# Attention into a routed expert layer: value rows copied by DMA instead of VectorE, and the first expert products planned together with the attention

## The chip, the cores and the metric

One core of a Trainium2 chip runs the whole program. The metric is the time of one execution on the device in microseconds, the median of several runs. Engines are named as in the profile: PE (TensorE), DVE (VectorE), ACT (ScalarE), POOL (GpSimd) and SP (SyncE, which only issues DMAs here).

## The reference, cut to what matters

The program has three parts in a row: an attention with a window, a layer of 8 experts of which each token uses one, and a gated layer. The change touches the first and the seam to the second.

```python
# attention: B, H, S, D = 4, 8, 768, 64; n_global, n_local = 8, 96
keep = (key < n_global) | ((rel >= 0) & (rel < n_local))      # rel = query - key
scores = where(keep, scale * q @ k.T + bias, -1e9)            # bias falls with the distance
a = exp(scores - max); a = a / (sum(a) + 1e-9)
x = (a @ v) laid out as [3072 tokens, 512]
# experts: w1 is [8, 512, 1024], w2 is [8, 1024, 512]
logits = x @ w_gate;  expert_idx = argmax;  gate_w = its softmax probability
out[tokens of e] = gate_w * (relu(x_e @ w1[e]) @ w2[e])
# then: sigmoid(out @ w_gate2) * (out @ w_val) @ w_out
```

A query sees the first 8 keys and the 96 keys up to itself, so a tile of 128 queries needs the 8 global keys, 96 or more keys of the tile before it, and its own 128.

## The kernel before, in words

**Attention.** `attention` (L457) works through 24 tiles of 128 queries, 6 for each of 4 batches (tile t is row block i = t % 6 of its batch), each in two halves s = 2t and 2t + 1 of four heads. Per tile SP loads k, q and v (L489, L497); PE transposes k and q (T, L523); ACT or DVE copies them out of PSUM (TH, L534, L536). Per half, PE makes the scores (QK, L556), DVE adds the bias and takes the row's extreme (TTR, L566), ACT exponentiates (EXP, L583), PE transposes the weights (PT, L595), ACT and DVE (or POOL) split them into two float16 parts (PHI L608, PLO L621), PE multiplies with the values (PV, L636 to L638), ACT moves the result out of PSUM (PO, L644) and POOL divides by the sum (NM, L664; the last two halves on DVE). POOL splits the values themselves into two float16 parts of `V[t]` (VP, L506 to L511).

**The old tile's value rows.** PV of a tile with i > 0 multiplies with two value tiles: `V[t-1]` and `V[t]`. In `V[t-1]` the first 32 rows must hold something else than the old keys: 24 rows of zeros (with a constant in row 0) and the 8 global rows. The kernel keeps them ready in `spec`, filled by one small DMA on ACT's queue per batch (in PO, L642), and DVE copies these 32 rows over the first 32 rows of `V[t-1]` (VB, L516), 20 times in all, before the tile's first PV.

**Routing in attention.** After a tile's two NM, PE transposes the rows (X, L674), ACT and DVE split them (XE L680, XL L683), PE multiplies with the gate's weights (L, L690), and a chain of small DVE, ACT and PE operations (MX, MB, EW, EX, MW, OH, CUM, POS, SL, EP, SI, RR) finds each token's expert and its place in that expert's list. OH (L729) is the one-hot row of the chosen expert; CUM (L732) adds it to the running counts, POS (L736, L737) multiplies with it. RR stores the tile's rows to DRAM (L756, SP), SC scatters its token numbers into the lists (L759, POOL).

**The head.** After tile 18 (`HEAD`), HC and HS find the expert that has most tokens so far, HV has SP read its number, load the first 256 token numbers of its list (L1005) and the first quarter of its weights (L1024); HG gathers those token rows (POOL, L1052); XG (L1064), XP (L1075), XA (L1086) and XD (L1090) scale, transpose and split them; WH (L1031) and WL (L1038) split the weights.

**The planner.** `plan` (L400) is a list scheduler in Python: from `graph`'s dependences, `COST`, `HOP`, `LAG` and a fixed priority `RANK` per kind of operation it simulates five engines and emits all operations in the order of their simulated starts. Every engine is a queue in order, so this order decides who waits behind whom. Loads of tile t + 2 are emitted by hand ahead of the first operation of tile t; so are the clears of DRAM buffers (L187 to L194).

**The seam.** The plan ends with the last tile's NM. The rest of that tile's routing is not planned: `g.tail` holds it in three pieces, which `ffn` calls around the first product `mm1(0, 0)`, along with the split of the second quarter of the weights (on POOL for p < 2, L1031). The loads of the second and third quarter are issued by hand at SC of tile 21. `ffn` then runs 9 items (two of 256 tokens for the first expert, then one for each other expert) in 8 steps each. A step is one group of 12 matmuls of `mm1` (L1140; ACT and DVE turn it into two float16 parts, L1144, L1145) and one of `mm2` (L1157); `mm1` of step n + 1 is emitted ahead of `mm2` of step n. At n = 2 `routing` finds all lists' lengths, at n = 2 and 3 the token numbers and rows of item 1 are fetched, which needs the last tile's scatter.

Of the kernel before, what the change touches and what calls it, by code (L numbers as in the profile page):

```python
# [8 lines left out]
F32 = mybir.dt.float32  # L9
# [11 lines left out]
E = 8  # L21
# [122 lines left out]
def constants(tc, g, tmp):  # L144
# [58 lines left out]
UNIT = dict(  # L203
    ND="D", NS="A", T="P", GC="G", QK="P", TTR="D", EXP="A", PT="P", PHI="A", PLO="D", PV="P",
    PO="A", SM="G", RC="D", NM="G", PG="G", HC="P", HS="D", HV="S", HG="G", XG="D", WH="G", WL="D", XP="P", XA="A", XD="D", X="P", XE="A", XL="D", L="P", MX="D", MB="D", EW="D", EX="A", MW="D", OH="D", CUM="D", POS="P",
    SL="D", EP="D", SI="D", RR="D", SC="G", VP="G", VB="D",
)
COST = dict(
    T=0.438, GC=0.21, PV=0.364, PO=0.268, SM=0.29, RC=0.09, NM=0.585, PG=0.59, X=0.438,
    XE=0.478, XL=0.6, L=0.303, MX=0.075, MB=0.29, EW=0.135, EX=0.244, MW=0.073, OH=0.3, CUM=0.19, POS=0.055,  # L210
    SL=0.075, EP=0.3, SI=0.073, RR=0.075, SC=1.17, VB=0.4, HC=0.03, HS=1.04, HV=0.01, HG=1.3, XG=0.6, WH=1.01,
    WL=1.3, XP=0.5, XA=0.478, XD=0.605,
)
SMALL = dict(MB=0.075, EP=0.075, OH=0.17, CUM=0.075, SM=0.09)
# [5 lines left out]
    T=-585.54, TH=-103.10, GC=-1092.71, QK=342.11, TTR=729.21, EXP=758.03, PT=347.71, PHI=1.34, PLO=247.24,  # L220
    PV=-729.22, SM=723.51, PO=130.74, RC=441.88, NM=-435.94, X=-229.91, XE=-436.15, L=386.67, MX=2161.16,
    EW=1001.43, EX=-1348.91, MW=105.77, OH=-1379.26, CUM=165.73, POS=-352.27, SL=-1123.54, EP=402.59, SI=-2894.64,
    RR=-1471.08, SC=328.83, VP=716.58, VB=-1236.17, HC=547.55, HS=-1259.72, HV=-973.76, HG=-355.21, XG=-407.53,
    WH=952.70, WL=1888.62, XP=-481.22, XA=-1266.94, XD=26.01, XL=776.35, MB=-892.16, PG=58.37, ND=-2151.11,
    NS=-1641.63,
)
PACE = 8.9592
ASIDE = ((1, 1), (3, 1))
DIRECT = ()
THU = ("AA", "AD")  # L230
LAG = dict(HS=1.0, HV=8.5, HG=5.0)
HEAD = 18
# [14 lines left out]
def graph():  # L247
# [13 lines left out]
    for t in range(NTILE):  # L261
# [12 lines left out]
        add(("VP", t, 2), [("VP", t, 1)], cost=1.12)  # L274
        if i:
            add(("VB", t), [("PV", 2 * t - 1, 1)] + ([("PO", 2 * t - 2)] if i == 1 else []))
            add(("GC", t), [("TH", t - i, 0), ("QK", 2 * t - 2), ("QK", 2 * t - 1)])
        for s in (2 * t, 2 * t + 1):
            add(
                ("QK", s), [("TH", t, 0), ("TH", t, 1)] + ([("GC", t)] if i >= 1 else []),  # L280
                bank=("S", 2), cost=0.93 if i else 0.57,
# [13 lines left out]
            for z in range(2):  # L295
# [11 lines left out]
                else:  # L307
# [4 lines left out]
                    [("PLO", s, z), ("VP", t, 2)] + ([("VB", t)] if i else []) + ([("PV", s, 0)] if z else []),  # L312
# [15 lines left out]
        if t == NTILE - 1:  # L328
            break
# [5 lines left out]
        add(("MB", t), [("MX", t)])  # L335
# [3 lines left out]
        add(("OH", t), [("MW", t)])  # L339
        prev = [("CUM", t - 1)] if t else []  # L340
        add(("CUM", t), [("OH", t)] + prev)
        add(("POS", t), [("OH", t), ("EX", t)] + prev)
        add(("SL", t), [("POS", t)], [("L", t, 0)])
        add(("EP", t), [("EX", t)])
# [6 lines left out]
    add(("HV", t), [("HS", t), ("SC", t)])  # L351
    for z in range(2):
        add(("HG", t, z), [("HV", t)])
        add(("XG", t, z), [("HG", t, z)])
        add(("WH", t, z), [("HV", t)])
        add(("WL", t, z), [("WH", t, z)])
# [25 lines left out]
def plan():  # L382
# [3 lines left out]
    def rank(k):  # L386
# [3 lines left out]
        r = PACE * k[1] + RANK[op]  # L390
        if op in ("T", "TH"):
            return r + 3.0 * k[2]
# [16 lines left out]
    lands = {("T", 0): 4.1, ("T", 1): 5.8, ("VP", 0): 7.3, ("ND", 128): 4.6}  # L409
# [45 lines left out]
def attention(ctx, tc, g):  # L455
# [12 lines left out]
    spec = [v_p.tile([G0 + NG, H, 130], F16, name=f"spec{n}", bufs=1) for n in range(2)]  # L468
# [15 lines left out]
    def load(t):  # L484
        b, i = tiles[t]
        rows = slice(i * 128, (i + 1) * 128)
        for src, dst, nm in ((g.k, kn, "kn"), (g.q, qn, "qn")):
            x = dst[t] = qk_p.tile([128, H, D], F32, tag=nm, name=nm)
            nc.sync.dma_start(out=x, in_=src[b, :, rows, :].rearrange("h p d -> p h d"))  # L489
            if t == 0 and nm == "kn":  # L490
                for n, a in enumerate((g.n_global, g.n_local)):
                    nc.sync.dma_start(
                        out=g.raw[:, n, :],
                        in_=a.rearrange("(o n) -> o n", o=1).bitcast(U32).to_broadcast([128, 2]),
                    )
# [3 lines left out]
    def VP(bank, t, z):  # L499
        b, i = tiles[t]  # L500
        if z == 0:
            if t < 2:
                nc.gpsimd.memset(spec[t].bitcast(F32), 0.0)
                nc.gpsimd.memset(spec[t][0:1, :, D : D + 1], 1.0 / PSC)
# [118 lines left out]
    def PV(bank, s, z):  # L623
# [5 lines left out]
        srcs = [V[t]] if i == 0 else [V[t - 1], V[t]]  # L629
# [10 lines left out]
    def PO(bank, s):  # L640
        if s % (2 * NB) == 0:
            nc.scalar.dma_start(out=spec[s // (2 * NB) % 2][G0:], in_=V[s // 2][:NG])  # L642
# [153 lines left out]

    def WH(bank, t, z):
        moe.whigh(z, 0)

    def WL(bank, t, z):  # L800
        moe.wlow(z, 0)
# [7 lines left out]
    def XD(bank, t, z):  # L809
# [5 lines left out]
        HC=HC, HS=HS, HV=HV, HG=HG, XG=XG, WH=WH, WL=WL, XP=XP, XA=XA, XD=XD, VP=VP, VB=VB, ND=lambda bank, w: distance(w), NS=lambda bank, w, qd: slopes(w, qd),  # L815
# [9 lines left out]
    for op, *at, bank in plan()[0]:  # L825
        if op == "VP" and at[0] >= 2 and at[1] == 0:
            clear(at[0] - 2)
        if op == "SC" and at[0] == NTILE - 3:
            tmps.close()
            moe.open("mw", 1)  # L830
            for p in range(1, 3):
                moe.wload(0, p)
                moe.wload(1, p)
# [4 lines left out]
    z = NTILE - 1  # L838

    def tail(*ops, bank=None):  # L840
        for f in ops:
            f(bank, z)
# [1180 lines left out]
```

## Time and profile before

| | us |
|---|---|
| median of 3 runs | 1010.46 (1010.03 to 1010.9) |
| profiled execution, its own time | 1016.85 |
| its span, first to last instruction | 1015.0 |
| PE busy | 966.7 (95%) |
| DVE busy | 740.2 (73%) |
| ACT busy | 513.8 (51%) |
| POOL busy | 432.8 (43%) |

The shares are means over stages with different limits: attention fills about the first 196 us, the experts go to about 505 us, the gated layer takes the rest. PE's busy time is modelled and counts each matmul's pipeline, so a PE at 95% is not at its peak.

### The profile page before, as it was taken

The numbers are of one execution on the slowest core, as the hardware profiler recorded it, in microseconds if no ns is written. First come the engines' busy times: TensorE is split into PE (matmuls) and PEld (weight loads), VectorE is DVE, ScalarE is ACT, GpSimd is POOL, SyncE is SP. The second block draws the span as 40 slices with busy tenths as digits, with TensorE's granted clock in tenths as the row PEclk, the third lists the DMA queues.
The fourth block names the chain that finished last, engine by engine and source line by source line (L and its number), as shares of the span: only waits on it lengthen the run. The fifth ranks groups of instructions, "written<-read, shape, count | busy, mean of one in ns | idle before, by whom it ended". The sixth has DMA issues, their size and how long they took to land.

```text
span 1015.0 us, 20665 instructions
## 1 busy us (share of the span) xinstructions
PE 966.7 (95%) x7793; PEld 678.8 (67%) x7793; DVE 740.2 (73%) x1625; ACT 513.8 (51%) x987; POOL 432.8 (43%) x537
## 2 busy tenths in 40 slices
PE   7999999689999999999999999999999999999994
PEld 5878777577555556666555588666876668766683
DVE  5999989965678789876867698445974459644693
ACT  6999989535556566656544453222621137121440
POOL 8878878640333335333778812224022240222102
PEclk9999999999999999999999999999999999999997
DMA  9877693367899999996677635552355514554031
GB/s 198 210 174 179 148 213 94 94 192 230 264 291 272 322 312 290 327 342 215 186 247 258 216 130 226 177 185 95 131 205 205 183 56 172 198 188 160 1 125 67
DMA packets 165699, 197.33 MB, mean 194 GB/s; under 512 B 88547, under 2 KB 129910, under 8 KB 165590
## 3 DMA queue, kind: packets, MB, share of 16 engines
q1 hardware_dynamic: 159990, 181.73, 57.5%
q0 software_dynamic: 5008, 14.11, 4.4%
q8 instruction: 63, 1.03, 0.4%
q14 instruction: 46, 0.38, 0.1%
q10 hardware_dynamic: 592, 0.08, 0.1%
HBM read 146.81 MB, written 49.23 MB: 193 GB/s over the span
## 4 chain that ended last, share of the span: by engine, by line
PE 41%; DVE 8%; issue 3%; DMA 2%; ACT 0%; another core or an unknown queue 0%; SPq 0%; POOLq 0%; POOL 0%; DVEq 0%; ACTq 0%
PE q L1370 30%; PE p L1455 10%; DVE h L1348 2%; DVE wk L1360 2%; PE acc L1157 1%; PE hp L1140 1%; DMA raw<-in_moe_w_gate_dram 1%; DVE wl L1038 1%; DVE yo L1290 1%; DMA raw<-yT 1%; DVE wk L1357 1%; DVE h L1417 0%; DMA wy<-wz 0%; DVE h L1403 0%
## 5 line engine op out<-in xcount | busy, mean ns | idle before, releaser
L1370 PE MATMUL q<-yo,set 128*128 128x384 f16 x2016 | 330.7, 326 | 2.8 <-DVE h L1417 2.8
L1370 PEld LDWEIGHTS <-set 128*128 128x128 f16 x2016 | 197.2, 98 | 135.1 <-issue 6.0
L1455 PE MATMUL p<-wy,wk 128*128 128x256 f16 x1404 | 154.1, 273 | 0.2 <-DVE wk L1357 0.2
L1455 PEld LDWEIGHTS <-wk 128*128 128x128 f16 x1404 | 137.3, 98 | 16.7 <-DVE wk L1357 0.4
L1140 PE MATMUL hp<-xT,wh 128*128 128x256 f16 (+7 forms) x576 | 136.6, 323 | 2.9 <-ACT xT L1086 1.5
L1421 POOL TENSOR_TENSOR h<-h,t 128x384 f32<-128x384 f32 x60 | 59.1, 998 | 152.3 <-DVE t L1417 137.2
L1391 ACT ACTIVATE u<-q 128x384 f32<-128x384 f32 x48 | 23.1, 482 | 161.1 <-PE q L1370 147.5
L1538 POOL DMA_INDIRECT out_dram<-o,idt x24 | 23.6, 983 | 178.2 <-DVE o L1506 122.9
L1140 PE MATMUL hp<-xT,wl 128*128 128x256 f16 (+7 forms) x288 | 93.3, 324 | 3.4 <-DVE wl L1038 3.3
L1038 DVE SCALAR_TENSOR_TENSOR wl<-wr,wh 128x1024 f16<-128x1024 f32 x64 | 84.3, 1317 | 14.8 <-ACT wh L1033 6.8
L1157 PE MATMUL acc<-hl,wh 128*128 128x256 f16 (+7 forms) x288 | 93.0, 323 | 0.2 <-DVE hl L1145 0.2
L1157 PE MATMUL acc<-hh,wh 128*128 128x256 f16 (+7 forms) x288 | 93.0, 323 | 0.0
L1157 PE MATMUL acc<-hh,wl 128*128 128x256 f16 (+7 forms) x288 | 93.0, 323 | 0.0
L1423 ACT ACTIVATE h<-h 128x384 f32<-128x384 f32 x72 | 37.4, 521 | 103.6 <-DVE h L1417 77.3
L583 ACT ACTIVATE pp<-tt,mall 128x232 f32<-128x232 f32 (+1 forms) x192 | 81.7, 474 | 4.1 <-DVE mall L566 4.0
L1157 PEld LDWEIGHTS <-wh 128*128 128x128 f16 x576 | 56.6, 98 | 35.2
L1140 PEld LDWEIGHTS <-wh 128*128 128x128 f16 x576 | 56.6, 99 | 34.2 <-issue 1.7
L1393 DVE TENSOR_TENSOR u<-q,u 128x384 f32<-128x384 f32 x48 | 26.8, 558 | 67.6 <-PE q L1370 67.6
L1144 ACT ACTIVATE hh<-hp 128x256 f16<-128x256 f32 (+7 forms) x72 | 34.5, 479 | 81.4 <-PE hp L1140 73.8
L566 DVE CUSTOM_DVE_ANT_0 tt<-s,nb 128x232 f32<-128x232 f32 (+1 forms) x192 | 64.2, 368 | 7.7 <-PE s L556 5.8
L1145 DVE SCALAR_TENSOR_TENSOR hl<-hp,hh 128x256 f16<-128x256 f32 (+7 forms) x72 | 39.1, 543 | 41.0 <-ACT hh L1144 40.1
L970 POOL TENSOR_TENSOR parts<-pair,parts 128x512 f16<-128x512 f32 (+1 forms) x24 | 34.2, 1424 | 72.5 <-ACT parts L969 72.5
(215 smaller groups left out, 1941.3 us busy)
## 6 DMA issues: line engine op xcount, KB each, us to landing
wr<-in_moe_w_dram SPq DMA_DIRECT2D x64, 512.0 KB
set<-us SPq DMA_DIRECT2D x36, 896.0 KB
wy<-wz SPq DMA_DIRECT2D x28, 768.0 KB
us<-set SPq DMA_DIRECT2D x12, 896.0 KB
kn<-in_k_dram SPq DMA_DIRECT2D x24, 256.0 KB
qn<-in_q_dram SPq DMA_DIRECT2D x24, 256.0 KB
vn<-in_v_dram SPq DMA_DIRECT2D x24, 256.0 KB
raw<-in_moe_w_gate_dram SPq DMA_DIRECT2D x12, 512.0 KB
```

Source lines behind the costliest of these rows:

```text
L566: nc.vector.tensor_tensor_reduce(out=tt[s][:, j, :w], in0=S_[s][j % 2][:, j // 2, :w], in1=g.nb[w][:, h, :], scale=-0.125, scalar=3.0e38, ...
L583: nc.scalar.activation(pp[s][:, j, 256 - w :], tt[s][:, j, :w], AF.Exp, bias=g.mall[:, t, h : h + 1], scale=-1.0)
L970: nc.gpsimd.tensor_tensor(lo, x[:, b : b + k, :], hi, op=ALU.subtract)
L1038: self.tc.nc.vector.scalar_tensor_tensor(lo, self.raws.pop((z, p)), WS[z], hi, op0=ALU.mult, op1=ALU.subtract)
L1140: nc.tensor.matmul(bk, a[:, k, fs], b[:, k, :], start=(m == 0), stop=(m == 11))
L1144: nc.scalar.activation(hh, bk, AF.Relu)
L1145: nc.vector.scalar_tensor_tensor(hl, bk, 0.0, hh, op0=ALU.max, op1=ALU.subtract)
L1157: nc.tensor.matmul(acc[i][dk], a[:, f % 2, d], b, start=(f == 0 and m == 0), stop=(f == NF - 1 and m == 2))
L1370: nc.tensor.matmul(bk, w[:, za, a, us], self.y[zy][:, y, u, :], start=(start and n == 0), stop=(n == 5), skip_group_check=not start,)
L1421: (V if last else G).tensor_tensor(at(half, tok), at(half, tok), d, op=ALU.mult)
L1423: A.activation(d, d, AF.Sigmoid, scale=1.0 / (YS * AS[0]))
L1455: nc.tensor.matmul(bks[t], w[:, za, j, 128 * t : 128 * t + 128], y[:, j, zy, :], start=(new and j == 0 and m == 0 and t != 1), stop=(j == ...
```

## The change

- VB is gone, and so is `spec`. Three buffers `prev` of 128 rows hold the zeros, the constant and the 8 global rows for good (POOL memsets at tiles 0, 1 and 2), and a new operation VC on SP copies rows 32 to 127 of `V[t]` into `prev[t % 3]` by DMA (20 times, 96 rows of 2080 bytes). For i < 3 a second DMA of 8 rows brings the global rows. PV reads `prev[(t-1) % 3]` in place of `V[t-1]`.
- OH is a `tensor_tensor` of two tensors, where it was a `tensor_scalar` with a column as scalar.
- The loads of `n_global` and `n_local` move from SP's queue (behind the first k) to ACT's queue (ahead of the gate's weights).
- The last tile's routing is planned; `g.tail` is gone.
- `HEAD` is 16. New planned operations: MO (closes the temporary pool, loads the second quarter of the weights), WH and WL for that quarter (WH on ACT), MW2 (loads the third quarter), and M1, HH and HL, the first 4 `mm1` groups of item 0 with their two float16 parts, into a pool `early`. `ffn` leaves these out and begins with `mm2(0, 0)`.
- The planner's costs and priorities change, with a second set `RANKL` for tiles from 20 on; QK's cost, for one, goes from 0.93 to 1.0.

```diff
@@ tables
+    for n, a in enumerate((g.n_global, g.n_local)):
+        nc.scalar.dma_start(
+            out=g.raw[:, n, :], in_=a.rearrange("(o n) -> o n", o=1).bitcast(U32).to_broadcast([128, 2])
+        )
     g.wl = tmp.tile([128, KD, E], F32, name="wl")
@@ constants of the plan
-LAG = dict(HS=1.0, HV=8.5, HG=5.0)
-HEAD = 18
+LAG = dict(HS=1.0, HV=8.5, HG=5.0, MO=9.0, VC=3.5)
+HEAD = 16
+PRE = 4
@@ graph
+        if i < NB - 1:
+            add(("VC", t), [("VP", t, 2)] + ([("PV", 2 * t - 3, 1)] if t >= 2 else []))
         if i:
-            add(("VB", t), [("PV", 2 * t - 1, 1)] + ([("PO", 2 * t - 2)] if i == 1 else []))
...
-                    [("PLO", s, z), ("VP", t, 2)] + ([("VB", t)] if i else []) + ([("PV", s, 0)] if z else []),
+                    [("PLO", s, z), ("VP", t, 2)] + ([("VC", t - 1)] if i else []) + ([("PV", s, 0)] if z else []),
...
-        if t == NTILE - 1:
-            break
...
+    add(("MO", t), [("VP", max(ZAT) + 2, 0), ("HV", t)])
...
+    for m in range(4):
+        add(("WH", t, m), [("MO" if m > 1 else "HV", t)], **({"unit": "A", "cost": 0.95} if m > 1 else {}))
+        add(("WL", t, m), [("WH", t, m)])
+    for z in range(2):
+        add(("MW2", t, z), [("WL", t, z)])
+    for f in range(PRE):
+        add(("M1", t, f), [("XD", t, 0), ("XD", t, 1), ("WL", t, f // 2 * 2)], bank=("M", 1))
+        add(("HH", t, f), [("M1", t, f)])
+        add(("HL", t, f), [("HH", t, f)], [("M1", t, f, 0)])
@@ attention
-    def VB(bank, t):
+    def VC(bank, t):
         b, i = tiles[t]
-        nc.vector.tensor_copy(V[t - 1][: G0 + NG], spec[b % 2])
+        w = prev[t % 3]
+        nc.sync.dma_start(out=w[G0 + NG :], in_=V[t][G0 + NG :])
+        if i < 3:
+            nc.sync.dma_start(out=w[G0 : G0 + NG], in_=prev[(t - 1) % 3][G0 : G0 + NG] if i else V[t][:NG])
...
-        srcs = [V[t]] if i == 0 else [V[t - 1], V[t]]
+        srcs = [V[t]] if i == 0 else [prev[(t - 1) % 3], V[t]]
...
-        ev(t, "OH").tensor_scalar(c["oh"], c["ew"], c["mw"], 1.0, op0=ALU.is_equal, op1=ALU.mult)
+        ev(t, "OH").tensor_tensor(c["oh"], c["ew"], c["mw"].to_broadcast([128, E]), op=ALU.is_equal)
...
+    def MO(bank, t):
+        tmps.close()
+        moe.open("mw", 1)
+        moe.early = moe.exs.enter_context(tc.tile_pool(name="early", bufs=1, side="right"))
+        for z in range(2):
+            moe.wload(z, 1)
@@ ffn
-    g.tail[0]()
-    mm1(0, 0)
-    moe.whigh(0, 1)
-    moe.whigh(1, 1)
-    g.tail[1]()
-    moe.wlow(0, 1)
...
-        if n + 1 < len(steps):
+        if PRE <= n + 1 < len(steps):
             mm1(*steps[n + 1])
-        if n == 0:
-            g.tail[2]()
-            moe.wlow(1, 1)
```

## Rows read from the trace of the kernel before

**Rows 1.** Busy time by stage: stage, its length, then each engine's busy us, PE clock, DMA share, GB/s.

```profile
46.00:124.00 78.00, 74.25 (x1035) 62.82 (x1035) 73.02 (x338) 72.42 (x191) 64.22 (x104) 1.00 0.72 157
124.00:196.00 72.00, 64.43 (x904) 53.35 (x903) 66.36 (x303) 61.41 (x162) 59.59 (x90) 1.00 0.59 150
196.00:204.00 8.00, 3.90 (x41) 3.18 (x42) 7.58 (x31) 1.90 (x7) 2.40 (x2) 0.70 0.16 57
204.00:257.00 53.00, 47.73 (x414) 40.30 (x413) 31.27 (x70) 23.80 (x45) 12.98 (x19) 0.95 0.72 223
```

**Rows 2.** Timeline of DVE at the seam: start us, length us, engine, line, operation.

```profile
195.86 0.41 DVE L664 TENSOR_TENSOR x<-po,d 128x256 f32<-128x256 f32 x1
...
207.18 0.42 DVE L1145 SCALAR_TENSOR_TENSOR hl<-hp,hh 128x256 f16<-128x256 f32 x1 [1.34 <-ACT hh L1144]
```

**Rows 3.** Timeline of PE from the seam to the third item.

```profile
203.38 1.09 PE L674 MATMUL xtp<-ident,x 128*128 128x128 f32 x4
204.27 0.42 PE L1140 MATMUL hp<-xT,wh 128*128 128x256 f16 x1
...
208.52 0.18 PE L736 MATMUL lg<-oh,tri 128*128 128x8 f16 x1 [0.18 <-DVE oh L729]
...
236.96 0.38 PE L1140 MATMUL hp<-xT,wh 128*128 128x256 f16 x2
...
239.58 0.38 PE L1140 MATMUL hp<-xT,wh 128*128 128x256 f16 x2
...
257.05 0.57 PE L1140 MATMUL hp<-xT,wh 128*128 128x480 f16 x2
```

**Rows 4.** Waits of PE, 190 to 262 us: who waited for whom, us, times, longest.

```profile
PE hp L1140 <- ACT xT L1086: 1.5, 1, 1.5
...
PE hp L1140 <- DVE wl L1038: 0.9, 1, 0.9
PE hp L1140 <- POOL wh L1031: 0.7, 1, 0.7
PE hp L1140 <- DVE xT L1090: 0.6, 1, 0.6
```

**Rows 5.** Waits of SP's queue, 196 to 240 us.

```profile
SPq L1005 <- DMA lst<-idall,si: 8.8, 1, 8.8
```

**Rows 6.** Groups of DVE, 124 to 196 us: shapes and count, busy us, mean ns, idle before.

```profile
L729 DVE TENSOR_SCALAR oh<-ew,mw 128x8 f16<-128x8 f32 x10 | 6.9, 711 | 0.0
L516 DVE COPY vv<-spec 32x1040 f16<-32x1040 f16 x8 | 4.3, 534 | 0.3 <-PE lg L737 0.3
```

**Rows 7.** Groups of DVE, 0 to 205 us.

```profile
L732 DVE TENSOR_TENSOR cum<-cum,oh 128x8 f16<-128x8 f16 x23 | 5.7, 249 | 0.0
...
L1038 DVE SCALAR_TENSOR_TENSOR wl<-wr,wh 128x1024 f16<-128x1024 f32 x2 | 2.4, 1212 | 0.0
L1064 DVE TENSOR_SCALAR xg<-x 128x512 f32<-128x512 f32 x2 | 1.7, 869 | 0.0
L1090 DVE SCALAR_TENSOR_TENSOR xT<-mxt,xT 128x512 f16<-128x512 f32 x2 | 1.4, 692 | 0.3 <-ACT xT L1086 0.2
```

**Rows 8.** Timeline of ACT, 207 to 216 us.

```profile
213.63 1.05 ACT L1033 ACTIVATE wh<-wr 128x1024 f16<-128x1024 f32 x1
```

**Rows 9.** Timeline of POOL: the end of a value tile's split (tiles 0 and 22).

```profile
13.37 1.12 POOL L511 TENSOR_TENSOR vv<-vn,vv 128x512 f16<-128x512 f32 x1
...
181.41 1.11 POOL L511 TENSOR_TENSOR vv<-vn,vv 128x512 f16<-128x512 f32 x1
```

**Rows 10.** Timeline of DVE: the copy of 32 rows for tiles 1, 13 and 23.

```profile
20.86 0.71 DVE L516 COPY vv<-spec 32x1040 f16<-32x1040 f16 x1
...
114.44 0.68 DVE L516 COPY vv<-spec 32x1040 f16<-32x1040 f16 x1 [0.88 <-DMA spec<-vv]
...
190.50 0.47 DVE L516 COPY vv<-spec 32x1040 f16<-32x1040 f16 x1
```

**Rows 11.** Timeline of ACT's queue: the small copy that the copy for tile 13 waits for.

```profile
109.21 0.66 ACTq L642 DMA_DIRECT2D spec<-vv  x1
```

More of the change, by code (lines that the diff above doesn't have):

```diff
@@ L334, in graph @@
         add(("MX", t), [("L", t)])
-        add(("MB", t), [("MX", t)])
+        add(("MB", t), [("MX", t)], **last)
         add(("EW", t), [("MX", t)])
@@ L338, in graph @@
         add(("MW", t), [("EW", t)])
-        add(("OH", t), [("MW", t)])
+        add(("OH", t), [("MW", t)], **last)
         prev = [("CUM", t - 1)] if t else []
-        add(("CUM", t), [("OH", t)] + prev)
+        add(("CUM", t), [("OH", t)] + prev, **last)
         add(("POS", t), [("OH", t), ("EX", t)] + prev)
         add(("SL", t), [("POS", t)], [("L", t, 0)])
-        add(("EP", t), [("EX", t)])
+        add(("EP", t), [("EX", t)], **last)
         add(("SI", t), [("SL", t)])
@@ L390, in rank @@
         r = PACE * k[1] + RANK[op]
+        if k[1] >= (2 * LATE if op in QUAD else LATE):
+            r += RANKL.get(op, 0.0)
         if op in ("T", "TH"):
@@ L467, in attention @@
     pps = [p_p.tile([128, 4, 256], F32, name=f"pp{n}") for n in range(3)]
-    spec = [v_p.tile([G0 + NG, H, 130], F16, name=f"spec{n}", bufs=1) for n in range(2)]
+    prev = [v_p.tile([128, H, 130], F16, name=f"prev{n}", bufs=1) for n in range(3)]
     kT = ctx.enter_context(tc.tile_pool(name="kt", bufs=1)).tile([128, 4, S], F32, name="kT")
@@ L837, in attention @@
         emit[op](bank, *at)
[L838 to L842, printed above, removed]
-    g.tail = [
-        lambda: tail(X, XE, XL, bank=[3]),
-        lambda: tail(L, MX, MB, EW, EX, MW, OH, CUM, EP, RR, bank=[7]),
-        lambda: tail(POS, SL, SI, SC),
-    ]
 def routing(tc, g, scratch):
@@ L1090, in xlow, with mm1, hhigh, hlow @@
         self.tc.nc.vector.scalar_tensor_tensor(xl, src, XS, xh, op0=ALU.mult, op1=ALU.subtract)
+    def mm1(self, i, f, b):
+        n = ITEMS[i][2]
+        wh, wl = self.wts[0, (i * NF + f) // 2]
+        bk = self.hp[i, f] = self.g.ps.tile([128, 512], F32, tag=f"b{b}", name="hp")[:, 0:n]
+        fs = slice(128 * (f % 2), 128 * (f % 2) + 128)
+        xh, xl = self.xT[i]
+        m = 0
+        for k in range(KD):
+            for a, b in ((wh, xh), (wh, xl), (wl, xh)):
+                self.tc.nc.tensor.matmul(bk, a[:, k, fs], b[:, k, :], start=(m == 0), stop=(m == 11))
+                m += 1
+    def hhigh(self, i, f):
+        n = ITEMS[i][2]
+        if (i, f) < (0, PRE):
+            x = [self.early.tile([128, n], F16, tag=f"{z}{f}", name=f"early{z}") for z in "hl"]
+        else:
+            x = [self.hid.tile([128, 512], F16, tag=f"h{z}", name=f"h{z}")[:, 0:n] for z in "hl"]
+        self.hs[i, f] = x
+        self.tc.nc.scalar.activation(x[0], self.hp[i, f], AF.Relu)
+    def hlow(self, i, f):
+        hh, hl = self.hs[i, f]
+        self.tc.nc.vector.scalar_tensor_tensor(hl, self.hp.pop((i, f)), 0.0, hh, op0=ALU.max, op1=ALU.subtract)
     def xprep(self, i, j):
```

109 lines of the change are left out of this document (52 added, 57 removed).

## The prediction, written before the changed kernel was built or run

> **What bounds the kernel now.** I began with the windows, the span cut by stage [rows 1]. The reader is to see two different attentions and a hole. From 46 to 124 us DVE (73.0 of 78 us) and ACT (72.4) are full together; from 124 to 196 us DVE alone is (66.4 of 72, ACT 61.4). Then, from 196 to 204 us, DVE works on (7.58 of 8 us) while PE has next to nothing (3.90, at a mean granted clock of 0.70, so partly at 1.2 GHz and not at 2.4, after a stretch with little to do). Next, the timelines at the seam. Attention's last product ends on DVE at 195.86 + 0.41 = 196.27 us [rows 2]; the first expert product starts on PE at 204.27 and the first matmul of 480 columns, the third item's, at 257.05 [rows 3]. So the seam, from the last product to the third item, lasts 60.8 us. From there on PE's work is what the planner's part of the program cannot touch; an earlier start there is an earlier end.
>
> How much of the 60.8 us is PE's work? Two groups of 12 matmuls take 239.58 - 236.96 = 2.62 us, one 1.31 [rows 3]. Before the third item PE runs 31 groups (8 + 8 of item 0, 8 + 7 of item 1): 40.6 us. Eight token transposes (2 + 2 + 4) at an estimated 0.44, the last tile's transpose, two gate products and small change add 4.9. That is 45.5, so 15.3 us are lost: about 6.5 ahead of 204.27, where only some 2 us of that work stands, and about 9 behind it. Of these 9, PE waits 1.6 for the second weight quarter (0.9 + 0.7) and 2.1 for item 1's tokens (1.5 + 0.6) [rows 4]; a mean clock of 0.95 over 53 us [rows 1] is 2.6 more; the rest is smaller gaps.
>
> **The change part by part.**
>
> *The seam.* Weights and tokens of the head item are now split inside attention, the first four groups have their place there, and the last tile's routing is in the order. What follows the last product is then: the transpose, a chain of XE, XL, L, MX to OH, and POS. In the trace this chain, transpose to POS, takes 208.52 - 203.38 = 5.1 us, with an expert group's matmuls in it [rows 3]. Four groups are 5.2 us, so PE can fill it; if they run earlier, the wait is real but the groups are off the path, which is the same sum. Work after the last product: 40.6 + 0.44 x 6 + 1.0 for transpose, gate and POS = 44.2, and 0.5 to get going. Lost in it: the 1.6 for weights go (their loads come some 40 us earlier), the low clock at the start goes (1 us), so from the old 9 at most 6.3 is left; at least the 2.1 for item 1's tokens stays, since that chain (scatter, list, gather, transpose) is the same. I take 4.5, nearer to the middle since SP's wait for the last scatter, 8.8 us [rows 5], starts earlier relative to the products but is not shortened. 44.2 + 0.5 + 4.5 = 49.2: **11.6 us saved**, between 9.8 and 14.0.
>
> *124 to 196 us, where DVE binds.* Removed: 8 copies of 32 rows, 4.3 us; 10 one-hots at 6.9 us [rows 6]. What a one-hot of two tensors takes, no row shows. The nearest is CUM, of two tensors of the same shape in SBUF: 0.249 us [rows 7]; at that price ten take 2.5. The ends are the old price (6.9) and 1.5 (0.15 each, an estimate for CUM without its waits). Added: 4 weight remainders at 1.212, 2 scalings (1.7), 2 token remainders (1.4) [rows 7], 4 HL at 0.42 [rows 2]: 9.6. Sum: 66.4 - 4.3 - 4.4 + 9.6 = 67.3. DVE's fill there is 66.4/72 = 92.2%; kept, the stage takes 73.0: **1.0 us lost**. At the old one-hot price it is 71.7, or 77.8 us at that fill, 5.8 lost; at 96% fill with the cheap one-hot 69.0, 3.0 saved. ACT gets two WH at 1.05 [rows 8] and HH and XA, six short ones not unlike HL: 61.4 + 4.8 = 66.2, which needs 71.3 us at its fill of 92.8% in the stage before [rows 1], so DVE stays first.
>
> The one-hot's price hangs on what DVE waits for inside the instruction: 0.711 us for eight columns [rows 6] against 0.249 [rows 7]. The Trainium skill, SBUF — State Buffer, section "Who interferes with whom", speaks against this part: a DVE instruction with two SBUF inputs still contends with a GpSimd instruction that reads SBUF, as the old one did in its two-port mode. By it alone the one-hot could stay at its old price, and the sum would be 4.8 us worse; CUM's row is such an instruction and shows part of the wait, not all.
>
> *46 to 124 us, where ACT is as full as DVE.* DVE sheds work, ACT sheds none, so the gain ends at ACT: 72.4 us of work at 95% fill take 76.2, **1.8 saved**; 0 if nothing packs better, 4.1 at 98%. PE's modelled 74.3 of 78 may end it earlier.
>
> *VC on SP's queue.* 20 copies of 200 KB and 12 small ones. Each has, from the value tile being ready to the old copy's place in front of PV: the first 20.86 - 14.49 = 6.4 us, the last 190.50 - 182.52 = 8.0 [rows 9, 10]; over all 20 pairs the mean is 9.8 and the first is among the narrowest. An SBUF to SBUF copy issued at 109.21 was waited for until about 114.4, 5.2 us [rows 10, 11]. So it is covered, barely in places; what covers it is the tile of lead that VP has. If that goes, PE's PV stops, and ACT, POOL and the next tile's buffers behind it. VC stands in SP's order with tile loads, row stores, clears, and now the head's work: HV's register read and list load, four weight loads of 512 KB at HV and MO, two at MW2. Old: all of that after the tile loads, where nobody waits. New, two tiles earlier: loads of the last tiles and VC 18 to 22 stand behind it. SP's wait for a scatter's landing can be 8.8 us [rows 5]. I take **1.0 us lost** once, between 0 and 4.
>
> *At nothing:* the ACT queue's two small loads (q leaves SP some 1 us earlier, but the first scores also need the bias tables; up to 1 saved, I take 0.5), the memsets on POOL at the start (they replace two others), the second half of PO's DMA issue on ACT, MX to SI of the last tile (small, same instructions).
>
> Sum: 11.6 - 1.0 + 1.8 - 1.0 + 0.5 = 11.9 us. Against the profiled execution: 1016.85, of which 1015.0 is its span, becomes 1005; it stood 6.4 us over the median of the runs shown, which I leave with the profile, so 1010.46 - 11.9 = **998.5 us**.
>
> **The rivals.**
>
> *B, attention packs tighter.* With DVE relieved and a new order, both stages reach 97%: 78 to 74.7 us (ACT) and 72 to 69.4 (DVE), and item 1's tokens are in time. 14.0 + 3.3 + 2.6 + 0.5 = 20.4: 990. For it: three engines over 92% now hinder each other. Against: so they still do.
>
> *C, the one-hot stays dear.* Then the late stage costs 5.8: 998.5 + 4.8 = 1003.3. For it: the old one's 0.711 [rows 6] is mostly waiting, and POOL, busy 59.6 of 72 us [rows 1], is as busy after. Against: CUM's 0.249 [rows 7], with the same kind of operands. By the rule of the Trainium skill named above (SBUF — State Buffer, "Who interferes with whom") this is how it comes out.
>
> *D, slower: the value copies land late.* Place: PV of the 20 tiles with an old tile. If each lands 10 us after its values are ready, ten pairs are short, by 25.7 us together (over the same 20 differences): 1024. It decides from about 8.6 us, where 12 us are lost. For it: 5.2 us seen for 16 KB in a busy stretch [rows 10, 11], and SP's one order for stores that wait for DVE. Against: most of the slack is 7 us and more.
>
> *E, the seam doesn't move.* The head's weights or tokens come late, PE stands in the order in front of M1, and attention's end slips by what the seam gains: 1010.5.
>
> **How the numbers follow.** Forecast 0.58, B 0.14, C 0.13, D 0.10, E 0.05. The forecast's own unknowns reach from 14.0 + 3.0 + 4.1 + 1.0 = 22.1 saved (988) to 9.8 - 5.8 - 4 = 0 saved, ends that don't fall together; C's 1003.3 with the lower seam (1.8 less) and half the loss on SP (1.5) is 1006.6. The range 988 to 1007 holds B, the forecast and C and leaves out D and E and little else. A measurement of this kernel can tell about 0.2%, 2 us, from no change: faster 0.86, same 0.04, slower 0.10.
>
> **What would show it.** Right: no gap like 196 to 204 us in PE's row; `mm2(0, 0)` within 7 us of the last product; the last product at 194 to 197 us; about 49 us from it to the third item; the one-hot at 0.15 to 0.4 us; hardly a PE wait for `prev`. Wrong: PV waits for DMA that sum to more than 3 us, an ACT or PE wait for `wr` or the gathered rows inside attention, the one-hot at 0.5 us or more, or a third item that starts later than 250 us.

## The result, and the profile after

The changed kernel is slower: 1018.27 us (median of 4 runs) against 1010.25 of the kernel before beside it, a ratio of 1.0085 (95% interval 1.0067 to 1.0104). I had forecast 998.5, range 988 to 1007.

The windows of the changed kernel, cut as [rows 1] (stage, length, busy us of PE, PEld, DVE, ACT and POOL, then clock, DMA share, GB/s):

```profile
46.00:124.00 78.00, 69.97 (x969) 60.04 (x968) 69.28 (x326) 68.63 (x182) 60.90 (x98) 0.98 0.84 200
124.00:196.00 72.00, 59.94 (x777) 51.89 (x776) 54.24 (x261) 55.16 (x145) 48.99 (x77) 0.91 0.65 169
196.00:204.00 8.00, 5.18 (x75) 4.53 (x74) 7.67 (x28) 6.99 (x17) 8.00 (x13) 0.91 0.22 66
204.00:257.00 53.00, 49.21 (x535) 43.93 (x534) 37.64 (x107) 28.02 (x58) 19.39 (x27) 0.98 0.61 185
```

Nothing is full any more: from 124 to 196 us DVE works 54.2 us where it worked 66.4, ACT 55.2 where 61.4, POOL 49.0 where 59.6. The stage does not have more work, it waits. The two marks of the seam, as [rows 2, 3] (timelines of DVE and of PE):

```profile
217.89 0.42 DVE L686 TENSOR_TENSOR x<-po,d 128x256 f32<-128x256 f32 x1
...
261.78 0.57 PE L1127 MATMUL hp<-xT,wh 128*128 128x480 f16 x2
```

Attention's last product ends at 218.31 us, 22 later than in [rows 2]; from there to the third item it is 43.5 us, 17 fewer than in [rows 3]. What attention lost is in the waits of 40 to 222 us (who waited for whom, us, times, longest):

```profile
DVE tt L590 <- PE s L580: 13.1, 16, 6.7
...
POOL lst L781 <- DMA idx<-lst: 9.4, 1, 9.4
...
PE po L660 <- DMA prev<-vv: 6.1, 5, 2.7
...
PE po L660 <- POOL ph L636: 4.6, 1, 4.6
...
PE lg L758 <- DVE oh L751: 4.2, 4, 2.1
```

Two of these come from what stands in a queue. The first, in SP's timeline (start, length, line, out<-in):

```profile
167.72 0.70 SPq L518 DMA_DIRECT2D vn<-in_v_dram  x1
168.47 1.04 SPq L538 DMA_DIRECT2D prev<-vv  x1
169.56 0.69 SPq L540 DMA_DIRECT2D prev<-vv  x1
170.35 0.38 SPq L778 DMA_DIRECT2D xd<-xr  x1
170.79 0.53 SPq L538 DMA_DIRECT2D prev<-vv  x1
173.02 0.68 SPq L540 DMA_DIRECT2D prev<-prev  x1
173.81 0.53 SPq L538 DMA_DIRECT2D prev<-vv  x1
175.66 0.70 SPq L540 DMA_DIRECT2D prev<-prev  x1
176.47 0.38 SPq L778 DMA_DIRECT2D xd<-xr  x1
178.26 0.43 SPq L1031 DMA_DIRECT2D idx<-lst  x1
```

The value load (L518) at 167.72 stood for GpSimd to free its buffer. Behind it stood three copies of 96 rows (L538) and their small copies (L540), of which two waited for the landing of the one before; the values of the first copy had been ready since 160.5. In SP's waits over the run the value loads wait longest of attention's transfers:

```profile
SPq L518 <- POOL vv L532: 23.6, 7, 6.9
...
SPq L518 <- POOL vv L527: 18.4, 3, 7.7
...
SPq L540 <- DMA prev<-vv: 3.5, 2, 1.9
...
SPq L540 <- DMA prev<-prev: 2.1, 2, 1.2
```

They had waited as long in the kernel before (SP's waits there):

```profile
SPq L497 <- POOL vv L511: 25.4, 8, 5.2
...
SPq L497 <- POOL vv L506: 13.8, 3, 7.2
```

There it cost nothing: from 40 to 200 us the engines waited 0.9 us in all for DMAs, VectorE once for the small copy of [rows 10].

The second, in POOL's timeline, is the list scatter of tile 17, placed right behind that of tile 16. It writes the list that the head's list load (SP, 178.26 above) reads, and so stands until that has landed:

```profile
170.52 1.04 POOL L781 DMA_INDIRECT lst<-idall,si  x1 [0.15 <-issue]
...
180.93 0.98 POOL L781 DMA_INDIRECT lst<-idall,si  x1 [9.37 <-DMA idx<-lst]
```

Behind it stand GpSimd's half splits, then TensorE's products, DVE and the head's gathers (189.71 us before, 193.28 now, though the head is tile 16 and no longer 18). The planner has no edge between the two scatters and the load: to it, tile 17's scatter can follow tile 16's at once.

The one-hots did not become cheap (groups of DVE, 124 to 196 us, as [rows 6, 7]):

```profile
L751 DVE TENSOR_TENSOR oh<-ew,mw 128x8 f16<-128x8 f32 x7 | 4.6, 656 | 0.1
...
L754 DVE TENSOR_TENSOR cum<-cum,oh 128x8 f16<-128x8 f16 x7 | 1.8, 253 | 0.1
```

### The profile page after: what moved, and what is told of

It reads as the page before. It is cut to its first block, busy times and chain, and to the rows that moved or that the text cites. A ratio compares the mean times of both kernels' runs of the same rounds, so it can differ in the third digit from the quotient of the medians.

```text
span 1016.2 us, 20649 instructions
## 1 busy us (share of the span) xinstructions
PE 964.8 (95%) x7793; PEld 684.6 (67%) x7793; DVE 734.0 (72%) x1605; ACT 516.8 (51%) x989; POOL 428.8 (42%) x537
## 4 chain that ended last, share of the span: by engine, by line
PE 69%; DVE 4%; issue 3%; DMA 1%; ACT 0%; POOL 0%; POOLq 0%; DVEq 0%
PE q L1400 30%; PE p L1485 13%; PE hp L1127 12%; PE acc L1196 12%; PE e L1508 1%; PE mxt L1101 1%; DVE h L1378 1%; DVE yo L1320 1%; DVE wk L1390 1%; DVE wl L1064 1%; DMA wy<-wz 0%; DMA x<-xd,idx 0%; DVE h L1447 0%; DVE h L1433 0%; DVE hl L1141 0%
## 5 line engine op out<-in xcount | busy, mean ns | idle before, releaser
L1196 PE MATMUL acc<-hl,wh 128*128 128x256 f16 (+7 forms) x272 | 88.2, 324 | 0.0
L1196 PE MATMUL acc<-hh,wh 128*128 128x256 f16 (+7 forms) x272 | 88.2, 324 | 0.0
L1196 PE MATMUL acc<-hh,wl 128*128 128x256 f16 (+7 forms) x272 | 88.2, 324 | 0.0
L607 ACT ACTIVATE pp<-tt,mall 128x232 f32<-128x232 f32 (+1 forms) x192 | 79.6, 476 | 3.3 <-DVE mall L590 3.0
L1059 ACT ACTIVATE wh<-wr 128x1024 f16<-128x1024 f32 x62 | 64.9, 1049 | 0.5 <-DMA wr<-in_moe_w_dram 0.5
```

The lines of the kernel that those rows point to most:

```text
L607: nc.scalar.activation(pp[s][:, j, 256 - w :], tt[s][:, j, :w], AF.Exp, bias=g.mall[:, t, h : h + 1], scale=-1.0)
L1059: self.tc.nc.scalar.activation(hi, raw, AF.Copy, scale=WS[z])
L1196: nc.tensor.matmul(acc[i][dk], a[:, f % 2, d], b, start=(f == 0 and m == 0), stop=(f == NF - 1 and m == 2))
```

## The experiments

All runs in one table. "Exps" are the softmax instructions of 192 begun by 167 us; "product" is the end of attention's last product, "store" the first expert result's store, both in us of the profiled execution. The chips differ (the kernel before took 1007.9 to 1014.4 us on them), so the paired ratio decides, and stage times are read to a few us. S, V and C in the table are the three edits shown below; the "theories" in the quoted expectations are rival explanations, and their letters have nothing to do with the edits.

| kernel | ratio to before (95%) | exps | product | store |
|---|---|---|---|---|
| before (first profile; again; third) | 1 | 166; 169; 167 | 196.3; 193.7; 194.6 | 237.7; 231.8; 232.6 |
| changed (first profile; again) | 1.0085 (1.0067–1.0104) | 162; 163 | 218.3; 217.0 | 242.4; 240.8 |
| S: late scatter | 1.0069 (1.0047–1.0091) | 158 | 216.2 | 242.8 |
| V: late value loads | 1.0066 (1.0049–1.0083) | 167 | 215.3 | 241.3 |
| no 96-row copies | 1.0062 (1.0040–1.0084) | 168 | 213.5 | 239.9 |
| S + C (small copies) | 1.0063 (1.0042–1.0084) | 161 | 217.3 | 241.3 |
| S + V | 1.0004 (0.9989–1.0018) | 168 | 206.8 | 230.7 |
| V + C | 1.0016 (1.0003–1.0028) | 173 | 207.4 | 231.3 |
| S + V + C | 0.9979 (0.9960–0.9998) | 168 | 205.0 | 229.2 |
| S + C, copies from ScalarE's queue | 1.0016 (0.9999–1.0033) | 161 | 210.9 | 235.1 |
| S + V + C, no 96-row copies | 0.9978 (0.9960–0.9996) | 168 | 206.1 | 233.0 |
| S + V + C, DVE's copies of before | 1.0026 (1.0007–1.0044) | 167 | 210.4 | 237.1 |
| S + V + C, old one-hots | 1.0006 (0.9993–1.0019) | 171 | 204.7 | 229.9 |
| S + V + C + gate on ScalarE (twice) | 0.9969 (0.9950–0.9989); 0.9985 (0.9970–1.0000) | 168; 170 | 204.7; 205.3 | 229.8; 229.2 |
| the same, late weight halves | 1.0032 (1.0019–1.0045) | 168 | 208.7 | 236.8 |
| the same, one-hots from PSUM | **0.9929 (0.9909–0.9949)** | 173 | 203.5 | 232.1 |

### Which wait? Scatter, value loads, copies

S, tile 17's scatter behind the head's gathers:

```diff
-    for op, *at, bank in plan()[0]:
+    todo = plan()[0]
+    late = [k for k in todo if k[:2] == ("SC", HEAD + 1)]
+    todo = [k for k in todo if k[:2] != ("SC", HEAD + 1)]
+    n = [k[:-1] for k in todo].index(("HG", HEAD, 1)) + 1
+    todo[n:n] = late
+    for op, *at, bank in todo:
```

> The changed kernel with one list scatter moved: that of tile 17 follows the head's two row gathers on GpSimd instead of following tile 16's scatter. Theory W (the loss is GpSimd standing 9.4 us at that scatter until the head's list load has landed, with all that queues behind it): the 9.4 us wait goes, softmax exps 174 and later come 5 to 9 us earlier, attention's last product ends at 209 to 213 us instead of 218.3, and the kernel takes 1009 to 1014 us. Theory Q (the loss is SyncE's queue, value copies late behind value loads, all through attention): the wait goes but the products wait elsewhere, 1016 to 1018 us. Theory O (the new planned order as such, too full on VectorE after 196 us): within 1.5 us of 1018.3.

The 9.4 us stand was gone, the time hardly moved (1.0069). TensorE still waited 4.9 us for copies, and attention was late without the stand (158 exps). Theory Q's case.

V, each value load issued where its buffer's last reader has been issued:

```diff
-        x = vn[t] = qk_p.tile([128, H, D], F32, tag="vn", name="vn", bufs=4)
-        nc.sync.dma_start(out=x, in_=g.v[b, :, rows, :].rearrange("h p d -> p h d"))
+        if t < 4:
+            vload(t)
...
             nc.gpsimd.tensor_tensor(V[t][:, :, D + 2 :], vn.pop(t), V[t][:, :, 0:D], op=ALU.subtract)
+            if t + 4 < NTILE:
+                vload(t + 4)
```

> The changed kernel with each value load issued only after its buffer's last reader has been issued on GpSimd, so that it no longer stands at the front of SyncE's queue for up to 7 us ahead of value copies and row stores. Theory Q: TensorE's 6.1 us of waits for the copied rows falls under 2 us, the 5 us that attention is late by 124 us shrink to 0 to 2, and the kernel takes 1012 to 1015 us. Theory W: the copies come earlier, but the scatter still stands about 9 us, 1016 to 1018 us. Theory O: within 1.5 us of 1018.3, or slower, since value loads land later.

Attention kept pace with the kernel before up to 167 us (167 exps), then stood 6.7 us at the scatter; 1.0066 is theory W's case. So each edit met the other cause. The third run, for the whole price of the copies, deletes the `dma_start` into `w[G0 + NG :]` and clears `prev` once:

> The changed kernel with the copies of 96 value rows left out (the previous tile's values are then zeros and the output differs; the small copies, the plan and every product stay). It gives the whole price of the copies, their DMA load and their waits. Theory Q: 4 to 8 us less, 1010 to 1014 us. Theory W: the products stop waiting for copies, the 9.4 us stand stays, 1 to 3 us less, 1015 to 1017 us. Theory O: under 1.5 us less.

Even without the copies 1.0062: attention on time at 167 us (168 exps), then 7.7 us at the scatter. The profile's row names VectorE for this stand, but the list load went out 2.5 us before its end, as in the change (2.7). The copies' data is not the cost.

All together, with C, the small copies read from the value tile:

```diff
-            nc.sync.dma_start(out=w[G0 : G0 + NG], in_=prev[(t - 1) % 3][G0 : G0 + NG] if i else V[t][:NG])
+            nc.sync.dma_start(out=w[G0 : G0 + NG], in_=V[t - i][:NG])
```

> The changed kernel with both edits of the two runs before it (late scatter of tile 17, value loads issued after their buffers come free), and the small copies read from the value tile of the batch's first token block instead of from the copy before, so that they wait for no landing. Theories W and Q each as sized by those runs: their savings add up, since one acts up to 170 us and the other from 171 us: 1004 to 1011 us. If they remove the same wait twice, no better than the better of the two. Theory O: within 1.5 us of 1018.3.

0.9979: 10.7 us less than the change (1.0085 - 0.9979 of 1010.25), the last product at 205.0. Three runs that each lack one edit:

> The run with both edits, with the small copies put back as the change has them (read from the copy before, so that each waits for the landing of the one ahead). Theory S (scatter and value loads both have to go, since each hides behind the other; the small copies matter little): within 2 us of the run with all three, attention's last product at 204 to 208 us. Theory T (the small copies' waits on SyncE are the second cause): attention's last product at 210 us or later, 1015 us or more.

> The changed kernel with the late scatter and with the small copies read from the value tile, value loads as the change has them. Theory S: the copies still stand behind value loads, attention's last product at 212 to 217 us, 1016 us or more. Theory T: nearly all of the gain of the three edits, last product at 204 to 208 us, within 2 us of that run.

> The changed kernel with the value loads issued late and the small copies read from the value tile, but tile 17's list scatter where the change has it. Theories S and T alike: up to 167 us as the run with all three edits (167 or 168 exps by then), then GpSimd stands 5 to 8 us at the scatter, the last product ends at 213 to 216 us, 1016 to 1020 us. If the scatter is harmless once SyncE's queue is free: last product at 204 to 208 us.

Without V little is gained (1.0063, an interval that overlaps the change's); with V, either of the others brings most of it (1.0004, 1.0016). Theory S had the first two about right (S + V came to 2.5 us, not 2, of the run with all three) and missed the third: with SP free the head's list load went out at 167.42, and the same stand, 6.2 us at 163.8, was largely taken up by the lead that attention then had (173 exps by 167 us). Of the three, the blocked value loads weigh most; scatter and small copies cost where they add to them.

Is it SP's queue, or the copies' data? The copies go through ScalarE's queue (both `nc.sync` in `VC` become `nc.scalar`), the value loads stay in the way on SP:

> The run with the late scatter and the small copies from the value tile (the products still waited 9.0 us for copies there, attention's last product ended at 217 us, first result store at 241.3 us), with the copies issued from ScalarE's queue instead of SyncE's; value loads stay where the change has them. If SyncE's in-order queue is the cause (copies stand behind value loads that wait for GpSimd): the waits for copies fall under 2 us and the run comes to where the late value loads brought it, last product 203 to 208 us, first result store 229 to 232 us, 1.000 to the kernel before within 0.002. If the copies are late because their transfers are slow or their sources late: as the run without this edit, 1.006.

1.0016, as V + C: the queue it was. Waits for copies fell from 9.0 to 2.1 us. Product and store came 3 us later than the expected ranges: ScalarE, which issues 25 of the copies between 40 and 200 us, is behind early (51 exps by 60 us, against 60 in S + C); that its issuing is the reason is not shown.

### What the copies are worth

> The run with all three edits, with the copies of 96 value rows left out (the previous tile's values are zeros in those rows and the output differs). Once SyncE's queue is free, the copies should cost nothing: last product within 1.5 us of 205.0 us and the time within 2 us of that run. If their transfers (4.5 MB in all) still crowd the queues: 2 to 5 us less.

0.9978 against 0.9979: with the queue free, 96-row copies cost nothing. And what they replace (the DVE copy emitted right after the old tile's last product):

```diff
+        if op == "PV" and at[0] % 2 and at[1] and at[0] // 2 + 1 < NTILE:
+            VB(at[0] // 2 + 1)
```

> The run with all three edits, with the copies of the kernel before put back: a VectorE copy of 32 rows into the old value tile, right after that tile's last product, and no copies of 96 rows. If my term for taking these copies off VectorE is right (18 copies of 0.53 us, 1.8 us of them in 46 to 124 us and more after it): 2 to 9 us slower than that run, last product at 207 to 214 us. If VectorE's copies were hidden, as SyncE's are: within 1.5 us of it.

0.47% or 4.7 us slower, last product 5.4 us later: taking the copies off DVE is a real gain, inside the expected 2 to 9. The plan does not know of the copies put back, so part of it may be their place in the order.

### The one-hots, and the rest of attention's end

In S + V + C the last product still ends 10 to 11 us after that of the kernel before. The loss now stands in one place: the last softmax instruction ends at 187.9 us (189.1 and 190.0 in the further profiles of before, 201.4 in the change), and from there to the last product it is 17.2 us, in the change 16.9, in all three profiles of before 4.6. The windows from one to the other in before's third profile, the change and S + V + C (columns as above):

```profile
190.00:194.60 4.60, 2.90 (x55) 2.33 (x52) 4.53 (x20) 2.25 (x7) 3.71 (x4) 1.00 0.56 143
```

```profile
201.40:218.30 16.90, 13.45 (x200) 12.22 (x200) 16.33 (x46) 9.88 (x22) 13.01 (x14) 0.90 0.25 73
```

```profile
187.90:205.00 17.10, 13.56 (x200) 12.38 (x200) 16.11 (x47) 9.79 (x21) 12.32 (x14) 0.90 0.24 66
```

So the three edits took away what was lost up to the last softmax instruction, and nothing of what is lost after it. There VectorE is nearly full, and 8.2 of its 16.1 us in S + V + C are the head's work (WL, XG, XD, HL). The runs below look for what sets this stretch.

> The run with all three edits, with the one-hots built as in the kernel before (one tensor, a scalar per row, two operations). If the form with two tensors is the dearer one beside GpSimd's work (its rows: 390 ns median, up to 3.1 us, against 524 and 1.2 before): the 22 one-hots take 1 to 4 us less in all, the kernel 0 to 3 us less. If both forms wait for the same reason: within 1 us of that run.

0.9979 and 1.0006 have overlapping intervals; the last product is at the same place. The old form's mean was longer (0.952 us over 40 to 205 us, against 0.730 for the new one there), its longest 5.37 us, so both wait.

> The run with all three edits, with the two gate products of the head (128 by 512, 1.32 and 0.47 us on VectorE) done by ScalarE. From 183 to 206 us VectorE is never idle by more than 0.7 us at a time there, so the 1.8 us should come off: last product at 202 to 204 us, 1 to 2 us less. If ScalarE's queue holds them up instead (it runs exps and copies there): 0 to 2 us more.

```diff
-        if i == 0 and UNIT["XG"] == "D":
+        if i == 0 and UNIT["XG"] == "A":
```

0.9969, last product 0.3 us earlier and not 1 to 2: no more than the spread of this kernel's two series. I still took the rest for DVE's amount of work, and moved two of the head's weight halves and a weight load behind the last product (`("WL", HEAD, 1)`, `("WL", HEAD, 3)`, `("MW2", HEAD, 1)` after `("NM", 2 * NTILE - 1)`):

> The run with the three edits and the gate products on ScalarE, with two of the head's four weight halves (those of the second weight, 1.2 us each on VectorE, needed only by the second products) moved from ahead of attention's last product to right behind it. Theory V (VectorE's queue sets attention's end): the last product ends 2.0 to 3.0 us earlier, at 201.5 to 203 us, and the first result store 0 to 2.5 us earlier, as far as the moved halves do not hold up the second products. Theory P (TensorE or the planned order sets it): last product within 0.7 us of that run, first result store 0 to 2 us later.

> The base of the run beside it, unchanged: last product at 204 to 206 us, first result store at 229 to 231 us, 0.995 to 0.999 to the kernel before.

Less work for DVE there, and the last product 3.4 to 4.0 us later than in the two profiles of the base: theory V fell. The timelines of POOL, DVE and PE of that run show what stands instead:

```profile
184.72 1.12 POOL L538 TENSOR_TENSOR vv<-vn,vv 128x512 f16<-128x512 f32 x1
185.80 1.16 POOL L651 TENSOR_TENSOR pl<-pf,ph 128x512 f16<-128x512 f32 x1
186.92 1.04 POOL L1074 TENSOR_SCALAR wh<-wr 128x1024 f16<-128x1024 f32 x1
187.91 0.10 POOL L533 MEMSET vv<- 128x16 f16 x1
187.97 0.61 POOL L534 TENSOR_SCALAR vv<-vn 128x512 f16<-128x512 f32 x1
188.56 1.03 POOL L1074 TENSOR_SCALAR wh<-wr 128x1024 f16<-128x1024 f32 x1
189.56 0.61 POOL L536 TENSOR_SCALAR vn<-vn 128x512 f32<-128x512 f32 x1
```

```profile
184.84 5.35 DVE L759 TENSOR_TENSOR oh<-ew,mw 128x8 f16<-128x8 f32 x1
```

```profile
190.24 0.19 PE L766 MATMUL lg<-oh,tri 128*128 128x8 f16 x1 [5.50 <-DVE oh L759]
```

A one-hot of eight columns, 0.15 us where nothing holds it, takes 5.35: it begins 0.12 us after the first of GpSimd's subtractions and ends at 190.19, with the last of a row of operations that leaves no pause (190.17). TensorE has the position product next in its order and stands 5.50 us. Then its clock is low (windows of that run, and of its base, which had the same 5.35 us one-hot at 183.19; columns as above):

```profile
185.00:190.00 5.00, 0.00 (x0) 0.00 (x0) 5.00 (x1) 3.81 (x8) 5.00 (x7) 0.95 0.13 40
190.00:194.00 4.00, 3.34 (x26) 3.22 (x27) 3.43 (x14) 0.97 (x2) 0.17 (x1) 0.50 0.00 0
194.00:199.00 5.00, 3.92 (x38) 3.50 (x37) 2.96 (x8) 3.27 (x8) 3.68 (x4) 0.50 0.08 8
```

```profile
190.00:194.00 4.00, 2.92 (x24) 2.50 (x22) 2.02 (x6) 2.37 (x7) 0.49 (x1) 0.66 0.00 0
194.00:199.00 5.00, 5.00 (x89) 4.83 (x90) 5.00 (x11) 3.90 (x8) 4.68 (x6) 1.00 0.35 108
```

With the halves moved TensorE stayed at 1.2 GHz until 199 us; with them in place it was back at 2.4 GHz from 194 us. That is where the loss up to the last product shows; why the clock rose sooner in one than in the other no run here tells. Another 4.2 us are lost behind that product: from there to the third item it is 47.6 us, in this base 43.4, and what holds it there was not traced. Nor does the 5.35 us one-hot set attention's end by itself: the other profile of the base has none above 3.06 us, and its last product comes at 204.7 us against 205.3.

The last run takes the one-hots out of GpSimd's way. The weighted mask is kept in PSUM, the counts are added on GpSimd:

```diff
-        c["ew"] = small(t, "ew", E)
+        c["ew"] = lg[t][:, 2 * E : 3 * E]
...
-        ev(t, "CUM").tensor_tensor(g.cum[(t + 1) % 4], g.cum[t % 4], chain[t]["oh"], op=ALU.add)
+        (nc.vector if t == NTILE - 1 else nc.gpsimd).tensor_tensor(g.cum[(t + 1) % 4], g.cum[t % 4], chain[t]["oh"], op=ALU.add)
```

> The run with the three edits and the gate products on ScalarE, with the weighted masks (ew) that the one-hots read kept in PSUM beside the logits, so that a one-hot has one large operand from PSUM as the products sl (0.15 us each in every run) have, and with the running counts added by GpSimd instead of VectorE. Theory C (small VectorE operations with all operands in SBUF wait until GpSimd pauses): one-hots fall to 0.15 to 0.25 us each, TensorE's waits for them from 9.3 us to under 1.5 us, attention's last product ends 4 to 9 us earlier than in the base (205.2 us), at 196 to 201 us, first result store at 221 to 226 us, 0.989 to 0.995 to the kernel before. Theory V (VectorE's amount of work in 186 to 205 us): under 1.5 us earlier. If GpSimd's counts come late and hold the positions instead: up to 3 us later.

0.9929 (0.9909 to 0.9949), by the ratios 4 to 6 us below its base and 7.2 us below the kernel before: it beats both kernels. Its groups and waits over 40 to 205 and 40 to 222 us:

```profile
L762 POOL TENSOR_TENSOR cum<-cum,oh 128x8 f16<-128x8 f16 x22 | 5.3, 242 | 8.6 <-DVE oh L759 5.2 <-PE xtp L704 2.4 <-DVE ep L776 0.9
...
L759 DVE TENSOR_TENSOR oh<-lg,mw 128x8 f16<-128x8 f32 x22 | 3.6, 162 | 1.0 <-ACT ex L747 0.6
```

```profile
PE po L668 <- DMA prev<-vv: 1.8, 1, 1.8
PE lg L766 <- DVE oh L759: 1.5, 4, 0.6
```

One-hots at 0.162 us each, TensorE's wait for them 1.5 us (5.7 and 9.3 in the two profiles of the base): theory C has the mechanism of the wait. Its price is less sure. The last product came at 203.5, not 196 to 201, and the first store at 232.1, 2 to 3 us behind the base. The exps lead the base (182 begun by 175 us against 177 and 180), but at the end the exponential of the logits waits for the mask, since both are in one PSUM tile (ACT ex <- DVE mw, 2.8 us once). The profiled execution was the slowest of its six (1009.7 us; the fastest took 1004.2), so it does not show where the gain lies. The gain over the base rests on ratios from different chips: beside this run the kernel before took 1013.5 us, beside the base's two series 1014.4 and 1008.5; against the second the medians are the same, 1007.2 us. And two things changed at once, the mask's place and the counts' engine; no run parts them.

### How typical the first profiles were

> The kernel before, unchanged, profiled again. If its first profile was long ahead of the experts: softmax exps reach 192 by 184 to 190 us, the last product ends at 188 to 193 us and the first result store comes at 231 to 235 us (237.65 in the first profile). If it was long behind that store: last product at 196 us, first store at 237 to 238 us, and less than 777 us from that store to the end (779.2 in the first).

> The kernel before, unchanged, a third profile, with the same two cases as the run ahead of it; with three profiles, the spread of the last product, of the first store and of the time from there to the end is told for each by itself.

> The changed kernel, unchanged, profiled again. Its first profile was at its own median. If the stand at the list scatter and the late copies are what this order of work brings, and no accident of one execution: a stand of 6 to 10 us there, 3 to 10 us of waits for copies, 160 to 164 exps at 167 us, last product at 215 to 220 us, first store at 240 to 244 us.

The first two further profiles are of the kernel before (timelines of DVE and PE, the marks of [rows 2, 3]), the third of the changed kernel (its waits):

```profile
193.32 0.41 DVE L664 TENSOR_TENSOR x<-po,d 128x256 f32<-128x256 f32 x1
...
251.19 0.57 PE L1140 MATMUL hp<-xT,wh 128*128 128x480 f16 x2
```

```profile
194.19 0.41 DVE L664 TENSOR_TENSOR x<-po,d 128x256 f32<-128x256 f32 x1
...
251.98 0.57 PE L1140 MATMUL hp<-xT,wh 128*128 128x480 f16 x2
```

```profile
POOL lst L781 <- DMA idx<-lst: 8.8, 1, 8.8
...
PE po L660 <- DMA prev<-vv: 5.7, 3, 3.2
```

The profile I had read was 5.1 to 5.9 us late at the first store: some 2 in attention and 3.4 in the seam, which is 57.4 us in both others, not 60.8. The changed kernel's losses repeat.

## Why the prediction was wrong

**The step that failed** is the term for VC on SP's queue, "1.0 us lost once, between 0 and 4". The three edits, all on that queue and on what waits for it, are worth 10.7 us. I had named the right cover (VP's lead, 6.4 us at the narrow end, 9.8 in the mean) and the right danger, that copies stand in SP's order with other work, but took only the head's part of that work as new. The value loads, which already waited up to 7.2 us for GpSimd before the change, stood ahead of the copies; no engine had waited for them there between 40 and 200 us. And I followed the list load only forwards, to the gathers, not to the scatter that may not overwrite its source: 9.4 us on GpSimd had no term.

**Seam**, forecast 11.6 saved. It shrank from 57.4 (typical) to 43.5 us, 13.9 saved, at the upper bound of 14.0; the base of 60.8 was one execution's. Taken alone the step held. But part of this was only moved: 24 of the head's expert matmuls (two groups, 2.6 us) and 8 us of DVE's work for it now run ahead of the last product. Seam and attention's end have to be read together: in S + V + C the third item starts at 248.6 us, against 251.2 and 252.0 in the further profiles of before.

**46 to 124 us**, 1.8 saved: 118 exps by 124 us instead of 124 to 126. With the three edits (123) it is about level with before, so the gain did not come either. Yet DVE's copies were worth removing: put back into S + V + C they cost 4.7 us, most of it after 167 us (173 exps begun by 175 us against 178).

**124 to 196 us**, 1.0 lost, is the second step that failed, and as large. Most of the 22 us went here and just after it. I had spread the head's 9.6 us of DVE work over the stage at DVE's usual fill of 92%; in the traces it stands nearly whole behind the last softmax instruction, where DVE is nearly full, and the stretch from there to the last product went from 4.6 to 16.9 us, 12.3 lost where 1.0 was forecast. The three edits left it at 17.2. I had also taken a one-hot at 0.249 us instead of 0.711 [rows 6, 7]; it measured 0.656 in the change, so next to none of the 4.4 us came. With the mask in PSUM the kernel became 4 to 6 us faster by the ratio, though its last product only 1 to 2 us earlier. What share of the 12.3 us is the head's work, its place in the order or the low clock, these runs do not settle; that DVE's amount of work alone does not set it, the late halves show.

Forecast and result are 20.5 us apart (11.9 saved, 8.6 lost by the ratio). The VC term was 9.7 too small and this one 11.3; the seam's 2.3 more than forecast go the other way.

**The rivals.** C's mechanism was in the result, with about its 4.8 us (4 to 6 by the ratio of the last run): the wait inside a one-hot also holds TensorE. The rule of the Trainium skill that stood beside it (SBUF — State Buffer, "Who interferes with whom": a DVE instruction with two SBUF inputs contends with a GpSimd instruction that reads SBUF) agrees with the 5.35 us row and with the 0.162 us of the same comparison from PSUM; the row of the counts, 0.249, on which I set it aside, was a mean of two kinds: in the trace of the kernel before a count takes 0.14 to 0.16 us where it waits for nothing and up to 0.62 us where it runs into a GpSimd operation. D had the sign, the nearest time (1024), the place and, among its reasons, SP's one order; it had stores that wait for DVE where the value loads waited for GpSimd, and nothing for the scatter or the head's work. E is out, the seam moved by 14 us. My range ended at 1007 with D and E alone beyond it.

**The marks** that I had set for "wrong": three of four showed, products waiting over 3 us for copies (6.1), a one-hot at 0.5 us or more (0.656), a third item after 250 us (261.78). The fourth did not: ahead of the last product no wait of PE or ACT is for `wr` or the gathered rows. The mark of the third item was a poor one: typical profiles of the kernel before start that item at 251.2 and 252.0. Startup and the small moves at nothing show no trace of their own.

## What to carry to other kernels

When a transfer that someone waits for joins an in-order queue, list what already stands in that queue and for whom it waits: a wait that cost nothing becomes the new transfer's. A hand-made plan needs the edges for overwriting as well as for reading; without them it puts an instruction where the engine must stand. When work moves ahead of a mark, read the stretches on both sides of it: the shorter one behind may have been paid for in front. And profile a kernel more than once before taking a stage's length from it.

## What the runs showed of the hardware

One VectorE operation on 128 by 8 elements with both operands in SBUF can last 5.35 us beside six back-to-back GpSimd operations of 0.6 to 1.2 us and a memset: it waited for the row of them to end. The old form, one tensor and a scalar per row, lasted 5.37 us in the same place. Not every one waits so long: in S + V + C a one-hot begun at 186.06 us took 1.01 and ended with the GpSimd operation that it had run into, though the next followed without a pause, and the gate product (1.32 us, 0.47 where GpSimd paused after its first 0.05 us) ended while a later one ran. What decides between the two is not shown. The same comparison with its large operand in PSUM took 0.154 to 0.167 us in all 24 cases, 13 of them begun while a GpSimd operation ran. The scatter of a tile's list took up to 7.0 us from issue to landing in the changed kernel, with 4.0 the median.
